# A spacer of 160 bytes in place of 32 on the right of SBUF, and longer durations in a static planner, in attention followed by two expert layers

## Chip, cores and metric

One core of one Trainium2 chip. The metric is the device time of one execution in microseconds, lower is better; three runs of the kernel before gave 1287.57, 1290.01 and 1291.79 us, and their median, 1290.01 us, is the time before.

## Reference

Three layers in a row, all in float32 (8 batches x 8 heads x 576 positions x 64; 4608 tokens, 512 wide):

```python
kv = einsum('bhsd,bhse->bhde', k, v); out = einsum('bhsd,bhde->bhse', q, kv)
x = (out / sqrt(mean(out * out, -1) + 1e-06) * g_norm)      # then heads side by side: 4608 x 512
h = x @ w_in;  g = h * cos(h);  x = g @ w_out               # first layer: 512 -> 2048 -> 512
h = x @ w_in2; solu = h * softmax(h)                        # second layer: 512 -> 1024
x = ((solu - mean(solu)) / sqrt(var(solu) + 1e-06) * g_ln) @ w_out2   # -> 4608 x 512
```

## The kernel before, in words

**Arithmetic.** Every float32 operand of the large products is held as a high and a low part in the format fp32r, side by side in one room, and a product is three matmuls (`mm3`): high by high (L171), high by low (L172), low by high (L173). The part that streams through TensorE, the moving operand, is 512 or 384 columns of 4 bytes; the stationary one is 128 x 128. `split` makes the parts (ACT writes the high one, L394 or L388; DVE or POOL the low one, L395 or L390), `cosine` makes g from h (ACT L667, DVE L669, ACT L672, DVE L674, ACT L676 for the high part, L677 on DVE or POOL for the low one). Inputs that come as pairs of 32-bit words are put together by `convert`: ACT L366, DVE L368, L370, L373, L375, POOL L377 (`either` picks the engine).

**Stages.** Phase 0 is 36 steps: in the gaps of the first quarter of the first layer lie the attention and the conversion of all weights, which go through the staging rooms `ws` out to DRAM (`wid`, `wod`; SP L402, L439). Phase 1 is 15 items, 5 blocks of tokens (384, 384, 512, 512, 512 columns) by the other 3 quarters of the hidden width: `first_h` computes h by seven products (moving operand `rxa` or `rxb`), `first_out` multiplies g (moving operand one of 12 `rg` rooms, taken in turn; rooms 8 to 11 are pieces of `rg2x`) by w_out. Each item's weights come back from DRAM into the left rooms `rwi` (L447) and `rwo` (L453, slots 0 and 1). The tokens of a block come by L726 into `xf`, and `prep` makes sums of them (POOL L627) and splits them into `rxa`/`rxb`. Phase 2 is 18 pairs of token tiles of the second layer; there `rxb` holds weights and is a moving operand too (L857).

**Rooms.** Pools are laid from the left end of SBUF upward (`const`, `rwo`, `rxa`, `rg`, `ws`, `fconv`, `sf`, `xf`, `fh`, then `pa` or `rwi`) and from the right end downward (`edge`, then `att`, later `rxb`, `mid`, `rg2`). `edge` is declared at L197 and opened first; no instruction reads or writes it, so its size only moves the other right rooms. In bytes within a partition the rooms on the left that this text speaks of start at 64 beyond a multiple of 256; `rxb` and `rg2x`, on the right, start at 192 beyond one (`rxb` at 204736, `rg2x` at 176064).

**The order.** Nothing is scheduled on the chip: each engine runs a fixed list. `Flow` collects tasks with an engine, a duration, a due time `at` and what they read and write, and `run` (L121) plays them through a small model. A ready task of the lowest due time goes first; a DMA lands a fixed 2.0 us after its end on the queue (`lat`); and all POOL tasks and all DVE tasks that don't read PSUM share one `port`, so in the plan only one of them runs at a time (L135, L150):

```python
return max(self.free.get(t.eng, 0.0), t.ready, port if t.port else 0.0)
...
if t.port:
    port = t.end
```

The durations are the second argument of each `add`. The order in which tasks start in the plan is the order of the program on every engine and queue, and semaphores make it right whatever the real durations are.

Of the kernel before, what the change touches and what calls it, by code (L numbers as in the profile page):

```python
# [11 lines left out]
U32 = mybir.dt.uint32  # L12
# [5 lines left out]
P = 128  # L18
# [48 lines left out]
class Flow:  # L67
# [13 lines left out]
    def declare(self, pool, tag, n, shape, dt=F32):  # L81

        for key in [(tag, i) for i in range(n)] if n else [tag]:
            self.pool_of[key] = pool
            self.specs.setdefault(pool, []).append((key, shape, dt))
# [18 lines left out]
    def add(self, eng, dur, fn, r=(), w=(), at=0.0, lat=0.0, ps=False):  # L104
        t = Task()
        t.eng, t.dur, t.fn, t.at, t.lat = eng, dur, fn, at, lat
        t.port = eng in ("POOL", "DVE") and not ps
        t.deps, t.next, t.end, t.left, t.seq = set(), [], None, 0, len(self.tasks)
        for k in {*r, *(self.pool_of[k] for k in (*r, *w) if k in self.pool_of)}:
            if k in self.writer:  # L110
                t.deps.add(self.writer[k])
            self.readers.setdefault(k, []).append(t)
        for k in w:
            t.deps.update(self.readers.get(k, ()))
            if k in self.writer:
                t.deps.add(self.writer[k])
            self.writer[k], self.readers[k] = t, []
        t.deps.discard(t)
        self.tasks.append(t)
# [40 lines left out]
def tile_kernel(ctx, tc, qkv, tail, g2, w1, w2, gl, out):  # L160
    nc = tc.nc
    PE, ACT, DVE, POOL, SP = nc.tensor, nc.scalar, nc.vector, nc.gpsimd, nc.sync
    flow = Flow()
    add = flow.add
    buf, declare = flow.buf, flow.declare

    def f(ap):
        return ap.bitcast(F32)
# [25 lines left out]
    declare("const", "ident", 0, [P, P])  # L194
    declare("const", "small", 0, [P, 2 * len(SMALL)])

    declare("edge", "edge", 0, [P, 8])  # L197
    for s in range(2):
        declare("rwi", ("rwi", s), 0, [P, 2 * NOP * 256], F32R)
        declare("rwo", ("rwo", s), 0, [P, 2 * 2 * 512], F32R)  # L200
# [96 lines left out]
    def rx(o, o_to=None):  # L297

        o_to = o + 1 if o_to is None else o_to
        if o < S1:  # L300
            room, at = buf["rxb"][:, 0:4096], o
        elif o == A22:
            room, at = buf["rxb"][:, 4096:6144], 0
        else:
            room, at = buf["rxa", (o - S1) // 2], (o - S1) % 2
        return room.rearrange("p (l c n) -> p l c n", l=2, n=512)[:, :, 2 * at:2 * (at + o_to - o), :]
# [41 lines left out]
    def e_(full, half, n):  # L348
        return half + (full - half) * (n - 256) / 256


    def convert(src, sk, yk, wk, at, load_at, on_dve, wide=1.3):
        def word(i):
            return buf[sk][:, :, i]

        def a():
            return buf[yk].bitcast(U32)

        if isinstance(src, list):
            for i, part in enumerate(src):  # L360
                add("SP", 0.8, lambda i=i, part=part: SP.dma_start(out=buf[sk][:, i * 256:(i + 1) * 256, :], in_=part),
                    r=[sk] if i else [], w=[("half", sk)] if i else [sk, ("half", sk)], at=load_at, lat=2.0)
        else:
            add("SP", 1.6, lambda: SP.dma_start(out=buf[sk], in_=src.rearrange("p (n w) -> p n w", w=2)),
                w=[sk, ("half", sk)], at=load_at, lat=2.0)
        add("ACT", 0.67, lambda: ACT.activation(out=buf[yk], in_=word(1).bitcast(F32), func=AF.Copy, scale=2.0 ** -112),  # L366
            r=[sk, ("half", sk)], w=[yk], at=at)
        add("DVE", 0.43, lambda: DVE.tensor_scalar(out=a(), in0=a(), scalar1=3, scalar2=None,  # L368
                                                   op0=ALU.logical_shift_left), r=[yk], w=[yk], at=at)
        add("DVE", 0.71, lambda: DVE.scalar_tensor_tensor(out=a(), in0=word(1), scalar=0x80000000, in1=a(),  # L370
                                                         op0=ALU.bitwise_and, op1=ALU.bitwise_or),
            r=[yk, sk, ("half", sk)], w=[yk], at=at)
        add("DVE", 0.43, lambda: DVE.tensor_scalar(out=buf[wk].bitcast(U32), in0=a(), scalar1=0xFF800000, scalar2=None,  # L373
                                                   op0=ALU.bitwise_and), r=[yk], w=[wk], at=at)
        add("DVE", 0.71, lambda: DVE.scalar_tensor_tensor(out=buf[wk], in0=word(0), scalar=2.0 ** -52, in1=buf[wk],  # L375
                                                         op0=ALU.mult, op1=ALU.mult), r=[wk, sk, ("half", sk)], w=[wk], at=at)
        either(on_dve, 512, lambda eng: eng.tensor_tensor(out=buf[wk], in0=buf[yk], in1=buf[wk], op=ALU.add),  # L377
               r=[yk, wk], w=[wk], at=at)

    def either(on_dve, n, fn, r, w, at):  # L380
        eng = DVE if on_dve else POOL
        dur = e_(0.8, 0.44, n) if on_dve else e_(1.2, 0.7, n)
        add("DVE" if on_dve else "POOL", dur, lambda: fn(eng), r=r, w=w, at=at)

    def split(src, keys, n, hi, lo, hk, lk, at, on_dve, scale=None):

        if scale is not None:
            add("ACT", 0.66, lambda: ACT.activation(out=hi(), in_=src(), func=AF.Copy, scale=scale()),  # L388
                r=[*keys, "gl"], w=hk, at=at)
            add("DVE", 0.71, lambda: DVE.scalar_tensor_tensor(out=lo(), in0=src(), scalar=scale(), in1=f(hi()),  # L390
                                                             op0=ALU.mult, op1=ALU.subtract),
                r=[*keys, *hk, "gl"], w=lk, at=at)
            return
        add("ACT", 0.64 if n == 512 else 0.42, lambda: ACT.copy(out=hi(), in_=src()), r=keys, w=hk, at=at)  # L394
        either(on_dve, n, lambda eng: eng.tensor_tensor(out=lo(), in0=src(), in1=f(hi()), op=ALU.subtract),  # L395
               [*keys, *hk], lk, at)
# [216 lines left out]
    def prep(src, keys, dst, hk, lk, at, lo_dve):  # L613

        fk = sfs()

        def sf(n, n_to=None):
            return buf[fk][:, 2 * n:2 * (n + 1 if n_to is None else n_to), :]

        def sk(n):  # L620
            return n, fk

        for n in range(4):
            flow.pool_of[sk(n)] = fk

        def op(out_, fn, in0, in1, r, w):
            add("POOL", 0.75, lambda: POOL.tensor_tensor(out=out_(), in0=in0(), in1=in1(), op=fn), r=[*keys, *r], w=w, at=at)  # L627

        a = src
        flow.change(lambda: None, (fk,), ())  # L630
        op(lambda: sf(0), ALU.add, lambda: a(1, 0, 2), lambda: a(1, 2, 4), [], [sk(0)])
        op(lambda: sf(1), ALU.subtract, lambda: sf(0), lambda: a(0, 0, 2), [sk(0)], [sk(1)])
        op(lambda: sf(2), ALU.subtract, lambda: a(0, 0, 2), lambda: a(1, 0, 2), [], [sk(2)])
        op(lambda: sf(3), ALU.subtract, lambda: a(0, 2, 4), lambda: sf(1), [sk(1)], [sk(3)])
        groups = [(0, 2, 512, lambda: a(0, 0, 4), []),
                  (2, 4, 512, lambda: sf(0, 2), [sk(0), sk(1)]),
                  (4, 6, 512, lambda: sf(2, 4), [sk(2), sk(3)]),
                  (6, 7, 256, lambda: a(1, 2, 4), [])]
        for n, (lo, hi, wide, s, r) in enumerate(groups):
            split(s, [*keys, *r], wide, lambda lo=lo, hi=hi: dst(0, lo, hi),  # L640
                  lambda lo=lo, hi=hi: dst(1, lo, hi), [(*hk, o) for o in range(lo, hi)],
                  [(*lk, o) for o in range(lo, hi)], at, lo_dve(n))
# [179 lines left out]
    def place_b(b):  # L822

        return {B11: A11, T2: S2, T1: S1, B21: A12, T3: S3, B22: S4, T4: A22}[b]
# [159 lines left out]
    def t_step(i):  # L984
        return T0 + STEP_A * i
# [7 lines left out]
    for i, (n, c) in enumerate(order):  # L993
        at = t_step(c + 2 * n) - CV_AHEAD
        wk = early_wf[i % 6]
# [64 lines left out]
    for i in range(NSTEP):  # L1060
        m, c = divmod(i, CPP)
        at, d = t_step(i), STEP_A
# [28 lines left out]
    at = T1_  # L1091
    for b, (t0, T) in enumerate(BLOCKS):

        for i, q in enumerate((3, 2, 1) if b % 2 else (1, 2, 3)):
            dur = e_(ITEM, ITEM / 2 + 0.6, T * P)
# [10 lines left out]
    for n, item in enumerate([*items, None]):  # L1106
        at = item["at"] if item else T_E2
        if item:
            T, q, dur = item["T"], item["q"], item["dur"]
# [10 lines left out]
        else:  # L1120
            dur, new = 22.0, True
# [5 lines left out]
            for b in (B11, T2, T1, B21, T3, B22, T4):  # L1127
                for kk in range(2):
                    for part in range(2):
                        add("SP", 0.8, lambda b=b, kk=kk, part=part: SP.dma_start(  # L1130
                            out=f(rx(place_b(b))[:, part, kk, :]).rearrange("p (z n) -> p z n", z=2),
                            in_=bd[:, kk, :, part, b * 256:(b + 1) * 256]),
                            r=[("bd", kk, 0, b), ("bd", kk, 1, b)] + ([("b", b)] if part or kk else []), w=[("b", b)],
                            at=at, lat=2.0)
# [17 lines left out]
    for c in range(NC):  # L1152
        flow.change(lambda: None, (f"rg{c}",), (f"lw{c}",))
        add("SP", 1.6, lambda c=c: SP.dma_start(out=f(rg(c)), in_=lwd[c]), r=[("lwd", c)], w=[("lw", c)],
            at=T_E2 + c, lat=2.0)
    for u in range(NU):
        at = T_E2 + 22 + PAIR_C * u
# [56 lines left out]
```

## Time and profile before

| | |
|---|---|
| median of 3 runs | 1290.01 us |
| profiled execution | 1292.3 us, of which the span is 1290.4 us |
| granted TensorE clock, mean | 0.989 |
| busy share of PE, DVE, ACT, POOL | 97%, 72%, 53%, 40% |
| PE on the chain that ended last | 75% |

All times of the trace count from the start of the span. PE's busy time has the modelled ends of pipelined matmuls in it, so the rate of a stretch is read from the starts of its instructions. A stretch in which PE waits shows in two views: in brackets behind the instruction that waited (the idle time, and the engine and line that ended it), and as busy time under the length of a window.

### The profile page before, as it was taken

How to read it: one execution, taken by the hardware profiler on the slowest of the kernel's cores; microseconds unless marked ns; L12 is line 12 of the kernel's file. 1: busy time of each engine (PE TensorE's matmuls, PEld its weight loads, DVE VectorE, ACT ScalarE, POOL GpSimd, SP SyncE). 2: the span in 40 equal slices, each digit the busy share in tenths (PEclk: the TensorE clock that was granted, in tenths of full speed). 3: DMA queues.
4: the chain of work that ended last, by engine and by line, in shares of the span. 5: the costliest groups of instructions: out<-in, count | busy, mean ns of one | idle time of the engine just before them, and what ended most of it. 6: DMA issues, size and time to landing. Idle time of an engine off the chain costs nothing.

```text
span 1290.4 us, 18723 instructions
## 1 busy us (share of the span) xinstructions
PE 1257.6 (97%) x6576; PEld 1066.5 (83%) x6576; DVE 930.3 (72%) x1544; ACT 677.9 (53%) x1225; POOL 518.3 (40%) x510
## 2 busy tenths in 40 slices
PE   5899999999999999999999999999999999999998
PEld 4688888887999899888788888887888888888887
DVE  6777777777887687878787766565777677776753
ACT  4666766675663563645364534442555545454533
POOL 2246656756745666554543443221321212121000
PEclk8899999999999999999999999999999999999999
DMA  8888899568948858663774374387111111111000
GB/s 278 292 264 283 286 326 304 191 216 282 336 152 227 285 184 276 211 227 115 241 221 157 101 212 136 107 284 237 59 56 50 50 42 56 43 50 42 25 25 33
DMA packets 177406, 224.59 MB, mean 174 GB/s; under 512 B 10912, under 2 KB 115360, under 8 KB 177312
## 3 DMA queue, kind: packets, MB, share of 16 engines
q1 hardware_dynamic: 177312, 223.39, 53.4%
q8 instruction: 52, 0.85, 0.3%
q14 instruction: 42, 0.34, 0.1%
HBM read 156.77 MB, written 66.58 MB: 173 GB/s over the span
## 4 chain that ended last, share of the span: by engine, by line
PE 75%; POOL 3%; DVE 3%; DMA 2%; issue 2%; ACT 1%; SPq 0%; POOLq 0%; ACTq 0%; DVEq 0%
PE ps L171 24%; PE ps L172 24%; PE ps L173 24%; PE ps L932 2%; POOL rg L677 1%; PE ps L552 1%; POOL fconv L419 1%; POOL fconv L377 1%; POOL ws L395 1%; DMA px<-fh 1%; PE ps L589 1%; DMA xf<-xd 0%; DMA bd<-ws 0%; PE ps L495 0%; DMA wid<-ws 0%
## 5 line engine op out<-in xcount | busy, mean ns | idle before, releaser
L171 PE MATMUL ps<-rg,rwo 128*128 128x512 f32 (+1 forms) x912 | 349.5, 383 | 1.6 <-ACT rg L676 1.6
L172 PE MATMUL ps<-rg,rwo 128*128 128x512 f32 (+1 forms) x912 | 346.6, 380 | 1.2 <-POOL rg L677 1.2
L173 PE MATMUL ps<-rg,rwo 128*128 128x512 f32 (+1 forms) x912 | 346.4, 380 | 0.0
L677 POOL TENSOR_TENSOR rg<-fh,rg 128x512 fp32r<-128x512 f32 (+1 forms) x120 | 149.3, 1253 | 174.4 <-ACT rg L676 161.5
L171 PEld LDWEIGHTS ps<-rg,rwo 128*128 128x128 f32 x912 | 171.9, 188 | 30.7 <-ACT rg L676 1.9
L172 PEld LDWEIGHTS ps<-rg,rwo 128*128 128x128 f32 x912 | 171.7, 188 | 30.3 <-POOL rg L677 2.2
L173 PEld LDWEIGHTS ps<-rg,rwo 128*128 128x128 f32 x912 | 171.6, 188 | 29.4
L914 POOL TENSOR_TENSOR const<-const,const 128x1 f32<-128x1 f32 x36 | 20.9, 580 | 333.2 <-DVE const L901 300.0
L171 PE MATMUL ps<-rxa,rwi 128*128 128x512 f32 (+1 forms) x384 | 147.3, 383 | 1.4 <-DVE fh L862 0.8
L172 PE MATMUL ps<-rxa,rwi 128*128 128x512 f32 (+1 forms) x384 | 145.6, 379 | 1.2 <-DVE rxa L395 1.2
L173 PE MATMUL ps<-rxa,rwi 128*128 128x512 f32 (+1 forms) x384 | 145.2, 378 | 0.0
L667 ACT ACTIVATE fh<-ps 128x512 int32<-128x512 f32 (+1 forms) x126 | 71.3, 567 | 103.4 <-PE ps L173 83.3
L672 ACT ACTIVATE fh<-fh,const 128x512 f32<-128x512 f32 (+1 forms) x156 | 106.6, 690 | 32.6 <-DVE fh L669 31.7
L171 PE MATMUL ps<-rxb,rwi 128*128 128x512 f32 (+1 forms) x288 | 112.7, 391 | 4.8 <-DVE fh L757 3.0
L676 ACT CAST rg<-fh 128x512 fp32r<-128x512 f32 (+1 forms) x156 | 90.6, 586 | 41.6 <-DVE fh L674 39.5
L173 PE MATMUL ps<-rxb,rwi 128*128 128x512 f32 (+1 forms) x288 | 110.4, 383 | 0.0
L172 PE MATMUL ps<-rxb,rwi 128*128 128x512 f32 (+1 forms) x288 | 109.9, 381 | 0.0
L669 DVE SCALAR_TENSOR_TENSOR fh<-ps,fh 128x512 f32<-128x512 f32 (+1 forms) x126 | 81.2, 648 | 28.3 <-ACT fh L667 25.6
L674 DVE TENSOR_TENSOR fh<-ps,fh 128x512 f32<-128x512 f32 (+1 forms) x126 | 80.9, 647 | 24.8 <-ACT fh L672 24.5
L627 POOL TENSOR_TENSOR sf<-xf 128x256 f32<-128x256 f32 x72 | 62.6, 876 | 61.9 <-DMA xf<-xd 32.5
L171 PEld LDWEIGHTS ps<-rxa,rwi 128*128 128x128 f32 x384 | 72.5, 189 | 14.5 <-DVE fh L862 1.3
L808 DVE TENSOR_TENSOR mid<-ps,mid 128x512 f32<-128x512 f32 (+1 forms) x90 | 56.9, 633 | 37.7 <-PE ps L173 37.2
(121 smaller groups left out, 2348.4 us busy)
## 6 DMA issues: line engine op xcount, KB each, us to landing
rwi<-wid SPq DMA_DIRECT2D x66, 512.0 KB, 5.7
rwo<-wod SPq DMA_DIRECT2D x88, 256.0 KB, 3.8
fconv<-w SPq DMA_DIRECT2D x36, 512.0 KB, 4.6
att<-qkv SPq DMA_DIRECT2D x32, 512.0 KB, 5.9
px<-fh SPq DMA_DIRECT2D x42, 256.0 KB, 4.2
xd<-xf SPq DMA_DIRECT2D x18, 512.0 KB, 3.9
wid<-ws SPq DMA_DIRECT2D x18, 512.0 KB, 4.7
xf<-xd SPq DMA_DIRECT2D x18, 512.0 KB, 5.2
```

The lines of the kernel that those rows point to most:

```text
L171: PE.matmul(ps, lhsT=lh, rhs=rh, start=start, stop=False, skip_group_check=more)
L172: PE.matmul(ps, lhsT=lh, rhs=rl, start=False, stop=False, skip_group_check=more)
L173: PE.matmul(ps, lhsT=ll, rhs=rh, start=False, stop=stop, skip_group_check=more)
L627: add("POOL", 0.75, lambda: POOL.tensor_tensor(out=out_(), in0=in0(), in1=in1(), op=fn), r=[*keys, *r], w=w, at=at)
L667: add("ACT", e_(0.61, 0.42, n), lambda: ACT.activation(out=tt().bitcast(I32), in_=h(), func=AF.Copy, scale=INV_2PI, bias=0.25), r=r, w=[tk ...
L669: add("DVE", e_(0.71, 0.44, n), lambda: DVE.scalar_tensor_tensor(out=tt(), in0=h(), scalar=INV_2PI, in1=tt().bitcast(I32), op0=ALU.mult, o ...
L672: add("ACT", e_(0.74, 0.5, n), lambda: ACT.activation(out=tt(), in_=tt(), func=AF.Sin, bias=buf["halfpi"][:, 0:1], scale=TWO_PI), r=[tk, " ...
L674: add("DVE", e_(0.71, 0.44, n), lambda: DVE.tensor_tensor(out=tt(), in0=h(), in1=tt(), op=ALU.mult), r=[*r, tk], w=[tk], at=t, ps=psrc)
L676: add("ACT", e_(0.64, 0.42, n), lambda: ACT.copy(out=hi(), in_=tt()), r=[tk], w=hk, at=t + 2)
L677: either(on_dve, n, lambda eng: eng.tensor_tensor(out=lo(), in0=tt(), in1=f(hi()), op=ALU.subtract), [tk, *hk], lk, t + 2)
L808: add("DVE", e_(0.71, 0.44, n), lambda ak=ak, bk=bk: DVE.tensor_tensor(out=buf[ak][:, 0:n], in0=buf[bk][:, 0:n], in1=buf[ak][:, 0:n], op=A ...
L932: PE.transpose(tr()[:, c, :], buf["h2", n][:, (4 * q + c) * P:(4 * q + c + 1) * P], buf["ident"])
```

## The change

Two things, neither of which adds an instruction or changes a sum. `edge` grows from 8 to 40 floats, so every other right room lies 128 bytes lower (`rxb` at 204608, `rg2x` at 175936: 64 beyond a multiple of 256, as on the left). And the planner gets longer durations for DVE L368, L370, L373, for `either` (L377, L395, L419, L677) and for the sums of `prep` (L627).

```diff
-    declare("edge", "edge", 0, [P, 8])                                        # L197
+    declare("edge", "edge", 0, [P, 40])
...
-        add("DVE", 0.43, lambda: DVE.tensor_scalar(out=a(), in0=a(), scalar1=3, scalar2=None,     # L368
+        add("DVE", 0.55, lambda: DVE.tensor_scalar(out=a(), in0=a(), scalar1=3, scalar2=None,
...
-        add("DVE", 0.71, lambda: DVE.scalar_tensor_tensor(out=a(), in0=word(1), scalar=0x80000000, in1=a(),     # L370
+        add("DVE", 0.78, lambda: DVE.scalar_tensor_tensor(out=a(), in0=word(1), scalar=0x80000000, in1=a(),
...
-        add("DVE", 0.43, lambda: DVE.tensor_scalar(out=buf[wk].bitcast(U32), in0=a(), scalar1=0xFF800000, scalar2=None,     # L373
+        add("DVE", 0.48, lambda: DVE.tensor_scalar(out=buf[wk].bitcast(U32), in0=a(), scalar1=0xFF800000, scalar2=None,
...
     def either(on_dve, n, fn, r, w, at):
         eng = DVE if on_dve else POOL
-        dur = e_(0.8, 0.44, n) if on_dve else e_(1.2, 0.7, n)
+        dur = e_(0.82, 0.5, n) if on_dve else e_(1.38, 0.8, n)
...
-            add("POOL", 0.75, lambda: POOL.tensor_tensor(out=out_(), in0=in0(), in1=in1(), op=fn), r=[*keys, *r], w=w, at=at)     # L627
+            add("POOL", 0.9, lambda: POOL.tensor_tensor(out=out_(), in0=in0(), in1=in1(), op=fn), r=[*keys, *r], w=w, at=at)
```

The second part moves instructions on every engine from early in phase 0 to the end of phase 1. Three places, in order of time.

DVE at the start of phase 1's second item, around 320 us (`ps6`, `ps1` are banks of PSUM into which PE next adds; `fconv` is the conversion's room). Before:

```order
L757 TENSOR_TENSOR fh_0_115<-ps0_0_167,fh_0_115 128x384
L757 TENSOR_TENSOR fh_0_115<-ps1_0_171,fh_0_115 128x384
L669 SCALAR_TENSOR_TENSOR fh_0_115<-ps7_0_195,fh_0_115 128x384
L757 TENSOR_TENSOR ps6_0_191<-ps6_0_191,fh_0_115 128x384
L757 TENSOR_TENSOR ps1_0_171<-ps1_0_171,fh_0_115 128x384
L669 SCALAR_TENSOR_TENSOR fh_0_115<-ps6_0_191,fh_0_115 128x384
L669 SCALAR_TENSOR_TENSOR fh_0_115<-ps1_0_171,fh_0_115 128x384
L373 TENSOR_SCALAR fconv_0_101<-fconv_0_101 128x512
L669 SCALAR_TENSOR_TENSOR fh_0_115<-fh_0_115 128x384
L375 SCALAR_TENSOR_TENSOR fconv_0_101<-fconv_0_101 128x512
```

Now:

```order
L669 SCALAR_TENSOR_TENSOR fh_0_115<-ps7_0_195,fh_0_115 128x384
L757 TENSOR_TENSOR fh_0_115<-ps1_0_171,fh_0_115 128x384
L373 TENSOR_SCALAR fconv_0_101<-fconv_0_101 128x512
L757 TENSOR_TENSOR ps6_0_191<-ps6_0_191,fh_0_115 128x384
L757 TENSOR_TENSOR ps1_0_171<-ps1_0_171,fh_0_115 128x384
L669 SCALAR_TENSOR_TENSOR fh_0_115<-ps6_0_191,fh_0_115 128x384
L669 SCALAR_TENSOR_TENSOR fh_0_115<-ps1_0_171,fh_0_115 128x384
L375 SCALAR_TENSOR_TENSOR fconv_0_101<-fconv_0_101 128x512
L669 SCALAR_TENSOR_TENSOR fh_0_115<-fh_0_115 128x384
```

L373, which writes `fconv` and must wait until POOL L395 has read it, now stands ahead of the two L757 that hand `ps6` and `ps1` back to PE, and not behind them.

SP, the last conversion of w_out for the first block, around 392 us (`wod` is written from the staging rooms by L439 and comes back as `rwo` by L453; the two last L439 write what slot 1 then reads). Before:

```order
L361 DMA fconv_0_101<-w1 128x512 x3
L439 DMA wod_60<-ws_1_97 128x4x128 x2
L453 DMA rwo_0_75<-wod_60 128x512
L453 DMA rwo_1_76<-wod_60 128x512
L453 DMA rwo_0_75<-wod_60 128x512
L453 DMA rwo_1_76<-wod_60 128x512
```

Now:

```order
L439 DMA wod_60<-ws_0_96 128x4x128 x2
L453 DMA rwo_0_75<-wod_60 128x512
L361 DMA fconv_0_101<-w1 128x512
L453 DMA rwo_0_75<-wod_60 128x512
L361 DMA fconv_0_101<-w1 128x512
L439 DMA wod_60<-ws_1_97 128x4x128 x2
L453 DMA rwo_1_76<-wod_60 128x512
L726 DMA xf_1_111<-xd_58 128x1024
L453 DMA rwo_1_76<-wod_60 128x512 x3
```

The last pair of L439 stood ahead of all eight reloads (two more pairs of L453 follow there); now it stands behind those of slot 0 and straight ahead of the first reload of slot 1, `rwo_1`. In the combined order PE has 16 matmuls of 384 columns left between the last L439 and its first read of `rwo_1`.

ACT around 421 us, in an item of 384 columns. Before:

```order
L672 ACTIVATE fh_0_115<-fh_0_115,const_1_67 128x384
L667 ACTIVATE fh_0_115<-fh_0_115 128x384
L366 ACTIVATE fconv_0_101<-fconv_0_101 128x512
L676 CAST rg2_0_2491<-fh_0_115 128x384
L667 ACTIVATE fh_0_115<-ps7_0_195 128x384
L667 ACTIVATE fh_0_115<-ps6_0_191 128x384
L769 COPY fh_0_115<-ps0_0_167 128x384
L394 CAST ws_1_97<-fconv_0_101 128x512
L394 CAST ws_0_96<-fconv_0_101 128x512
```

Now:

```order
L672 ACTIVATE fh_0_115<-fh_0_115,const_1_67 128x384
L667 ACTIVATE fh_0_115<-fh_0_115 128x384
L667 ACTIVATE fh_0_115<-ps7_0_195 128x384
L676 CAST rg2_0_2449<-fh_0_115 128x384
L769 COPY fh_0_115<-ps0_0_167 128x384
L667 ACTIVATE fh_0_115<-ps6_0_191 128x384
L672 ACTIVATE fh_0_115<-fh_0_115,const_1_67 128x384 x3
```

The conversion's L366 is gone from ahead of L676, the cast that PE waits for, and the two L394 after it are gone as well; the next L366 now stands ten rows behind that L676.

## Rows read from the trace of the kernel before

**Rows 1.** the page: busy time of each engine, its share of the span, instructions

```profile
PE 1257.6 (97%) x6576; PEld 1066.5 (83%) x6576; DVE 930.3 (72%) x1544; ACT 677.9 (53%) x1225; POOL 518.3 (40%) x510
```

**Rows 2.** waits of PE: who waits for whom, us in total, times, longest

```profile
PE ps L171 <- DVE fh L757: 3.0, 1, 3.0
PE ps L171 <- ACT rg L676: 1.6, 1, 1.6
PE ps L172 <- POOL rg L677: 1.2, 2, 1.0
```

**Rows 3.** timeline of PE, 559 to 572 us: start, duration, instruction (512-wide products)

```profile
559.88 0.39 PE L171 MATMUL ps<-rxa,rwi 128*128 128x512 f32 x1
...
563.28 0.40 PE L171 MATMUL ps<-rxb,rwi 128*128 128x512 f32 x1
...
566.07 0.39 PE L171 MATMUL ps<-rg,rwo 128*128 128x512 f32 x1
...
568.16 0.40 PE L171 MATMUL ps<-rxa,rwi 128*128 128x512 f32 x1
```

**Rows 4.** the same, 413 to 426 us (384-wide products)

```profile
416.31 0.33 PE L171 MATMUL ps<-rxa,rwi 128*128 128x384 f32 x1
...
417.87 0.34 PE L171 MATMUL ps<-rxb,rwi 128*128 128x384 f32 x1
...
419.98 0.34 PE L171 MATMUL ps<-rg,rwo 128*128 128x384 f32 x1
```

**Rows 5.** groups by line and form: count, busy us and mean ns, idle before

```profile
L171 PE MATMUL ps<-rg,rwo 128*128 128x512 f32 x720 | 284.3, 395 | 0.0
...
L171 PE MATMUL ps<-rxb,rwi 128*128 128x512 f32 x216 | 88.1, 408 | 3.0 <-DVE fh L757 3.0
...
L171 PE MATMUL ps<-rg,rwo 128*128 128x384 f32 x192 | 65.1, 339 | 1.6 <-ACT rg L676 1.6
...
L171 PE MATMUL ps<-rxb,rwi 128*128 128x384 f32 x72 | 24.7, 343 | 1.8 <-DVE fh L674 1.2 <-ACT fh L769 0.6
```

**Rows 6.** timeline of PE, 628 to 648 us (in brackets: idle before it)

```profile
637.37 0.40 PE L173 MATMUL ps<-rxb,rwi 128*128 128x512 f32 x1
640.77 0.79 PE L171 MATMUL ps<-rxb,rwi 128*128 128x512 f32 x1 [3.01 <-DVE fh L757]
```

**Rows 7.** windows: length, busy PE, PEld, DVE, ACT, POOL, granted clock, DMA share, GB/s

```profile
307.00:323.00 16.00, 13.00 (x69) 11.46 (x68) 12.35 (x22) 8.54 (x18) 10.34 (x10) 1.00 0.98 303
415.00:426.00 11.00, 8.37 (x44) 7.80 (x43) 6.06 (x11) 5.11 (x11) 10.84 (x12) 0.95 0.75 217
641.00:647.00 6.00, 6.00 (x15) 4.68 (x16) 3.50 (x6) 4.33 (x8) 0.56 (x2) 0.52 1.03 358
```

**Rows 8.** timelines of POOL and of ACT, 628 to 648 us

```profile
632.91 0.74 POOL L627 TENSOR_TENSOR sf<-xf 128x256 f32<-128x256 f32 x1 [3.47 <-DMA xf<-xd]
...
634.93 0.72 ACT L388 ACTIVATE ws<-fconv,const 128x512 fp32r<-128x512 f32 x1 [11.22 <-POOL fconv L377]
```

**Rows 9.** DMA issues: count, KB each, median us from issue to landing

```profile
rwo<-wod SPq DMA_DIRECT2D x88, 256.0 KB, 3.8
...
wid<-ws SPq DMA_DIRECT2D x18, 512.0 KB, 4.7
...
wod<-ws SPq DMA_DIRECT2D x24, 256.0 KB, 4.7
```

**Rows 10.** groups by line and form, of the conversion's small pieces

```profile
L373 DVE TENSOR_SCALAR fconv<-fconv 128x512 uint32<-128x512 uint32 x42 | 23.9, 569 | 6.5 <-POOL ws L395 6.1
...
L395 POOL TENSOR_TENSOR ws<-fconv,ws 128x256 fp32r<-128x256 f32 x10 | 7.4, 737 | 20.1 <-ACT ws L394 20.1
...
L394 ACT CAST ws<-fconv 128x256 fp32r<-128x256 f32 x10 | 4.0, 404 | 13.7 <-DMA bd<-ws 8.5 <-DMA wid<-ws 5.0
```

**Rows 11.** groups by line and form, of L370 in the two conversion rooms

```profile
L370 DVE SCALAR_TENSOR_TENSOR fconv<-fconv 128x512 uint32<-128x512 uint32 x42 | 33.9, 808 | 0.5
...
L370 DVE SCALAR_TENSOR_TENSOR pa<-pa,pa 128x512 uint32<-128x512 uint32 x2 | 1.4, 690 | 0.0
```

## Prediction

> **What bounds the kernel.** I read the busy times first: PE works 1257.6 of 1290.4 us [rows 1], so 32.8 us of idleness is all that a better order can win, and two levers are left: what one matmul takes, and the few places where PE waits. The waits of PE between 300 us and the end are single events [rows 2]: one wait of 3.0 us for DVE L757, one of 1.6 us for ACT L676, one of 1.0 us for POOL L677. Then I read, from the starts of matmuls, what one takes. At 560 us 15 matmuls with `rxa` as moving operand start in 3.40 us, 227 ns each; the next 12, with `rxb`, take 2.79 us, 232.5 ns each; the 9 behind them take 2.09 us, 232 ns each, though not all of those read a room on the right [rows 3]. With 384 columns it is 1.56 us for 9 of `rxa`, 173 ns each, and 2.11 us for 12 of `rxb`, 176 ns each [rows 4]. So a moving operand from the right costs 2.5% or 1.5% more, and for a few matmuls after it the rate stays low.
>
> **The spacer.** It moves the right rooms from 192 to 64 beyond a multiple of 256 bytes, where the left ones lie. If the place within 256 bytes makes the difference, every right matmul falls to the left rate. How many are there? `rxb` has 216 per line with 512 columns and 72 with 384, on three lines: 648 and 216. Of `rg`, phase 1 has 864 matmuls of 512 columns and 576 of 384 (192 per line on three lines) [rows 5]; the twelve rooms are taken in turn and four are on the right, a third: 288 and 192. The last block of phase 0 reads its tokens from `rg2x`, 48 more. That is 984 x 5.8 ns = 5.7 us and 408 x 2.5 ns = 1.0 us; for the matmuls that stay slow after them I add an estimated 1.3 us (some 220 at 5.8 ns: a few after each right stretch, as in [rows 3]). Term: **-8.0 us**; bounds 0, if the place is not the cause, and -10, if more trail behind.
>
> **The order: what goes.** At 637 us DVE stands in L390, which waits for the conversion's ACT L388; L388 idled 11.22 us behind POOL L377, which stood behind a `prep` sum L627 that waited 3.47 us for its tokens [rows 8]. PE's next matmul starts 3.40 us after the one before it instead of 0.23, so 3.2 us are lost [rows 6]; then 15 matmuls in 6 us at a granted clock of 0.52, the lower of the two levels, instead of 3.4 us, 2.6 more [rows 7]. Now L390 is not near that place and L377 stands on the other side of the wait: **-5.8** (bounds -5.8 and 0, if the next late conversion takes its place). At 421 us L366 and the L677 behind it cost 11 - 8.37 = 2.6 us of PE, and the clock there is 0.95, 0.5 more [rows 7]; the conversion has moved away: **-3.1** (bounds -3.1 and 0).
>
> **The order: what comes.** The longer durations raise the load of the planner's common port for POOL and DVE. The trace's means hold waiting for the other engine: L370 takes 808 ns in the room `fconv`, when POOL converts too, and 690 ns in `pa` [rows 11]. The plan already keeps the two apart, so that time is counted twice; conversion work is planned later, and nearer to its due.
>
> First, 307 to 323 us. PE loses 16 - 13 = 3.0 us there already [rows 7]. Now L373 stands ahead of the two L757. It waits for a POOL L395 of 256 columns, that for ACT L394, and this for the landing of a `wid` transfer out of the staging room, 4.7 us after its issue [rows 9]; such waits cost POOL 20.1 us over ten pieces before, off the path [rows 10]. From that issue to the point where PE needs `ps6`, PE has 20 matmuls of 173 ns in the combined order, 3.5 us. So PE waits 4.7 - 3.5 + 0.40 + 0.74 + 0.57 [rows 10] and an L757 of about 0.55, an estimate from L373 itself: 3.5 us. An L677 on DVE that moved behind L669 and L368 ahead of the first products costs up to 2.5 us more, an estimate from three DVE steps near 0.6 each and ACT between them. A pause of that length is followed at 641 us by 2.6 us of loss from the clock; half of it here, since the pieces are shorter: 1.3. Together 3.5 + 2.5 + 1.3 beside what is lost now: **+7.3** (bounds 0, if DMA lands early, and +10).
>
> Second, 392 us, where PE never waited. The last L439 is issued 16 matmuls of 173 ns, 2.8 us, before PE's first read of `rwo_1`; it lands after 4.7 us, and only then can the reload be issued, which lands after 3.8 [rows 9]. PE waits 4.7 + 3.8 - 2.8 = 5.7 us, and then runs at the lower clock; 2.3 us of that by the nearest row, the 2.6 at 641 us: **+8.0** (bounds 0, if the conversion runs ahead of the plan, and +9).
>
> Third, late in phase 0, an L394 of 256 columns now waits for a `wid` landing ahead of the ACT copies that free PE's banks; 4.7 us [rows 9], of which the matmuls between cover most: **+1.0** (bounds 0 and +3.5). Everything else that moved I cost at nothing: it lies on DVE, ACT or POOL, which are idle 28%, 47% and 60% of the time [rows 1]; where that cover is gone, a wait like the ones above appears, up to 3 us each.
>
> **Sum.** -8.0 - 5.8 - 3.1 + 7.3 + 8.0 + 1.0 = -0.6 us. The profiled execution of 1292.3 us becomes 1291.7; it stood 2.3 us above the median of 1290.0, and against that the forecast is **1289.4 us**. Two large gains and two large losses cancel nearly; a measurement of this kernel tells about 0.3%, 3.9 us, from no change.
>
> **Rivals.** *The new waits mostly don't come* (faster). Each rests on a DMA landing at its median and on an engine that is as late as the plan has it; the plan before also took 2.0 us for transfers that need 3.8 to 4.7 [rows 9], and yet PE waited at few places [rows 2]. If half of the 16.3 us comes, the sum is -8.8: 1281 us. It speaks against this that both places put a transfer and its reader within 3.5 us of PE's work.
>
> *The place within 256 bytes does nothing* (slower). Left and right rooms also differ in how high they lie, and in that `rxb` and `rg2x` lie beside the sums that DVE writes in `mid`; in the trace all left rooms have one place and all right rooms the other, so it can't be split there. The matmuls of [rows 3] that read left rooms at the slow rate behind `rxb` speak a little for this. Price: the -8.0 is gone, the sum +7.4, 1297 us; it decides as soon as less than 3.5 of the 8 us come, which is right matmuls above 230 ns. The Trainium skill, in "SBUF — State Buffer", section "Specifications (TRN2)", gives lines of 16 bytes within which an access costs no more, and "SBUF: two separate sides" says that TensorE's port waits for nobody; by these, both spacers being multiples of 16, the move changes nothing and the time is this rival's. The 232.5 against 227 ns show that some difference between the rooms exists which those sentences don't name.
>
> *Neither part does what it says*: no gain from the rooms, and few of the new waits. Then -8.9 from what goes and +8 from what comes: within 0.3%.
>
> **Numbers.** Forecast (rooms gain, new waits come) 0.36; new waits mostly missing 0.30; rooms gain nothing 0.20; neither 0.10; a wait elsewhere that I have not seen 0.04. Faster by over 0.3%, under 1286.1: the second, and a tenth of the first, 0.34. Slower, over 1293.9: the third, the last, and 0.03 of the first, 0.27. The rest, 0.39, is within. The forecast's own range is 1285 to 1295; with the rivals, and the bounds of the two large new waits, 1278 to 1300.
>
> **What would show it.** Right matmuls (`rxb`, late `rg`) at 227 and 173 ns between starts; no wait of PE for L757 at the old 637 us and none at 421 us; a wait of PE on L171 to L173 for `rwo<-wod` near 392 us, followed by a stretch at a clock near 0.5; more than 3 us lost around 320 us. The prediction is wrong if `rxb` stays at 232 ns, or if PE passes 392 us without a pause.

## Result and the profile after

The change made the kernel slower: 1296.87 us (median of 6 runs, 1294.03 to 1298.25) against 1289.22 us for the kernel before (6 runs), a ratio of 1.0063 with a 95% interval of 1.0046 to 1.0079, so 8 us more. The forecast was 1289.4 us and no change that can be measured. The profiled execution has a span of 1295.3 us and a granted clock of 0.986 (before 1290.4 us and 0.989).

The busy times, which answer to [rows 1], and the waits of PE, which answer to [rows 2]:

```profile
PE 1250.2 (97%) x6576; PEld 1067.8 (82%) x6576; DVE 927.6 (72%) x1544; ACT 679.4 (52%) x1225; POOL 518.9 (40%) x510
```

```profile
PE ps L589 <- DVE att L584: 6.3, 5, 2.0
PE ps L171 <- DMA rwo<-wod: 6.2, 2, 3.5
PE ps L171 <- DVE fh L674: 5.9, 1, 5.9
...
PE ps L172 <- DVE rg L677: 2.9, 1, 2.9
PE ps L172 <- POOL rg L677: 2.1, 1, 2.1
PE ps L552 <- ACT xf L593: 1.7, 2, 0.8
PE ps L495 <- ACT xf L593: 1.6, 2, 0.8
```

PE is busy 7.4 us less than before although the span is 4.9 us longer: the matmuls became faster, the waits more. The wait of 3.0 us for L757 is gone. New, or far longer than before, are one of 5.9 us for L674, two for `rwo<-wod` of up to 3.5 us, two for L677 of 2.9 and 2.1 us, and four small ones for ACT L593.

How fast the matmuls became is read from the starts of PE's instructions (start, duration), as in [rows 3]:

```profile
575.32 0.39 PE L171 MATMUL ps<-rxa,rwi 128*128 128x512 f32 x1
...
578.04 0.39 PE L171 MATMUL ps<-rg,rwo 128*128 128x512 f32 x1
...
580.76 0.39 PE L171 MATMUL ps<-rxb,rwi 128*128 128x512 f32 x1
...
583.48 0.39 PE L171 MATMUL ps<-rg,rwo 128*128 128x512 f32 x1
```

Each of the three stretches has 12 matmuls in 2.72 us, 226.7 ns each. `rxb`, on the right, now runs like `rxa`; it took 232.5 ns before.

Where PE lost time, in windows that answer to [rows 7] (the same columns), all four of the changed kernel: at the first attention tiles, around the first item of phase 1, at the reads of `rwo`, and over the stretch in which PE had stopped at 637 us:

```profile
70.00:90.00 20.00, 16.97 (x144) 13.94 (x142) 13.64 (x24) 11.61 (x21) 6.42 (x6) 0.83 0.65 210
305.00:345.00 40.00, 27.82 (x133) 24.60 (x132) 23.65 (x36) 18.36 (x37) 27.66 (x28) 0.91 0.82 264
405.00:418.00 13.00, 6.80 (x30) 5.90 (x29) 9.32 (x13) 0.92 (x2) 6.90 (x8) 0.77 0.65 227
...
620.00:660.00 40.00, 40.00 (x178) 33.15 (x177) 31.66 (x47) 14.43 (x26) 21.52 (x21) 1.00 0.88 271
```

In the kernel before, the first of these windows was almost full, and the clock in it was whole:

```profile
70.00:90.00 20.00, 19.85 (x170) 16.11 (x169) 15.91 (x27) 14.54 (x28) 5.92 (x6) 1.00 0.78 248
```

To compare kernels whose instructions stand in another order, I worked out a **loss by stage** from the starts of PE's matmuls: the time from each start to the next, less 226.7 ns (512 columns) or 173.4 ns (384) for a matmul of L171 to L173; the rest, the attention's matmuls and the transposes included, counts whole. Stages end at the same number of matmuls of L171 to L173 in every kernel; the times in the head of the table are those of the kernel before. One traced execution each, in us; it can lie some us from the median of its kernel (e5 3.6 below, e2 3.4 and the kernel before 3.1 above), so a difference of 1 or 2 us in the table says little:

| kernel | to 86 us | to 290 | to 333 | to 403 | to 436 | to 799 | to the end | sum |
|---|---|---|---|---|---|---|---|---|
| before | 53.1 | 49.4 | 4.9 | 1.2 | 4.9 | 11.7 | 37.5 | 162.8 |
| changed | 60.5 | 47.6 | 15.9 | 9.2 | 0.0 | 0.1 | 34.7 | 168.0 |
| e1 spacer alone | 53.0 | 49.2 | 4.7 | 0.3 | 2.5 | 7.6 | 34.4 | 151.8 |
| e2 durations alone | 60.5 | 47.9 | 16.8 | 8.8 | 0.2 | 4.6 | 37.9 | 176.8 |
| e5 only `prep` | 53.1 | 49.2 | 8.7 | 0.0 | 0.0 | 7.1 | 34.7 | 152.7 |
| e6 only DVE | 54.9 | 52.2 | 15.7 | 0.0 | 0.0 | 2.1 | 34.4 | 159.2 |
| e7 only `either` | 55.5 | 49.7 | 10.9 | 2.9 | 0.0 | 2.2 | 34.6 | 155.8 |
| e8 no port | 58.3 | 54.2 | 5.2 | 2.4 | 7.7 | 2.5 | 37.3 | 167.7 |
| e9 late only | 53.8 | 49.1 | 4.8 | 0.2 | 0.0 | 2.5 | 34.7 | 145.1 |
| e10 first eight old | 53.4 | 48.8 | 21.9 | 8.3 | 0.0 | 0.1 | 34.7 | 167.2 |
| e11 from item two | 53.6 | 49.3 | 7.9 | 0.9 | 3.9 | 1.0 | 34.7 | 151.3 |

### The profile page after: what moved, and what is told of

It reads as the page before. It is cut to its first block, busy times and chain, and to the rows that moved or that the text cites. A ratio compares the mean times of both kernels' runs of the same rounds, so it can differ in the third digit from the quotient of the medians.

```text
span 1295.3 us, 18726 instructions
## 1 busy us (share of the span) xinstructions
PE 1250.2 (97%) x6576; PEld 1067.8 (82%) x6576; DVE 927.6 (72%) x1544; ACT 679.4 (52%) x1225; POOL 518.9 (40%) x510
## 4 chain that ended last, share of the span: by engine, by line
PE 91%; DVE 2%; DMA 2%; POOL 2%; ACT 2%; issue 1%; SPq 1%; ACTq 0%; DVEq 0%; POOLq 0%
PE ps L171 28%; PE ps L172 28%; PE ps L173 28%; PE ps L932 2%; PE ps L552 2%; PE ps L495 2%; PE ps L589 1%; POOL att L570 1%; DMA att<-qkv 1%; DMA rwo<-wod 0%; DMA xf<-xd 0%; DMA wod<-ws 0%; POOL att L569 0%; DVE att L562 0%; DVE fh L669 0%
## 5 line engine op out<-in xcount | busy, mean ns | idle before, releaser
L171 PE MATMUL ps<-rg,rwo 128*128 128x512 f32 (+1 forms) x912 | 349.1, 383 | 6.2 <-DMA rwo<-wod 6.2
L173 PE MATMUL ps<-rg,rwo 128*128 128x512 f32 (+1 forms) x912 | 345.5, 379 | 0.0
L677 POOL TENSOR_TENSOR rg<-fh,rg 128x512 fp32r<-128x512 f32 (+1 forms) x120 | 148.8, 1255 | 148.5 <-ACT rg L676 123.6
L171 PEld LDWEIGHTS ps<-rg,rwo 128*128 128x128 f32 x912 | 172.0, 189 | 34.8 <-issue 3.7
L173 PEld LDWEIGHTS ps<-rg,rwo 128*128 128x128 f32 x912 | 171.9, 188 | 28.4
L171 PE MATMUL ps<-rxa,rwi 128*128 128x512 f32 (+1 forms) x384 | 146.6, 382 | 2.1 <-DVE fh L862 1.0
L173 PE MATMUL ps<-rxa,rwi 128*128 128x512 f32 (+1 forms) x384 | 144.7, 377 | 0.0
L672 ACT ACTIVATE fh<-fh,const 128x512 f32<-128x512 f32 (+1 forms) x156 | 105.7, 689 | 41.5 <-DVE fh L669 40.9
L676 ACT CAST rg<-fh 128x512 fp32r<-128x512 f32 (+1 forms) x156 | 89.8, 585 | 52.4 <-DVE fh L674 49.9
L171 PE MATMUL ps<-rxb,rwi 128*128 128x512 f32 (+1 forms) x288 | 111.2, 386 | 5.9 <-DVE fh L674 5.9
L172 PE MATMUL ps<-rxb,rwi 128*128 128x512 f32 (+1 forms) x288 | 108.7, 377 | 0.0
L173 PE MATMUL ps<-rxb,rwi 128*128 128x512 f32 (+1 forms) x288 | 108.7, 377 | 0.0
L669 DVE SCALAR_TENSOR_TENSOR fh<-ps,fh 128x512 f32<-128x512 f32 (+1 forms) x126 | 80.9, 648 | 30.5 <-ACT fh L667 28.8
L674 DVE TENSOR_TENSOR fh<-ps,fh 128x512 f32<-128x512 f32 (+1 forms) x126 | 80.8, 646 | 20.5 <-ACT fh L672 20.0
L395 POOL TENSOR_TENSOR ws<-fconv,ws 128x512 fp32r<-128x512 f32 (+1 forms) x52 | 67.1, 1298 | 51.7 <-ACT ws L394 41.9
L377 POOL TENSOR_TENSOR fconv<-fconv 128x512 f32<-128x512 f32 x40 | 54.0, 1350 | 83.4 <-DVE fconv L375 81.2
```

What stands on the lines that cost most here:

```text
L171: PE.matmul(ps, lhsT=lh, rhs=rh, start=start, stop=False, skip_group_check=more)
L172: PE.matmul(ps, lhsT=lh, rhs=rl, start=False, stop=False, skip_group_check=more)
L173: PE.matmul(ps, lhsT=ll, rhs=rh, start=False, stop=stop, skip_group_check=more)
L669: add("DVE", e_(0.71, 0.44, n), lambda: DVE.scalar_tensor_tensor(out=tt(), in0=h(), scalar=INV_2PI, in1=tt().bitcast(I32), op0=ALU.mult, o ...
L672: add("ACT", e_(0.74, 0.5, n), lambda: ACT.activation(out=tt(), in_=tt(), func=AF.Sin, bias=buf["halfpi"][:, 0:1], scale=TWO_PI), r=[tk, " ...
L674: add("DVE", e_(0.71, 0.44, n), lambda: DVE.tensor_tensor(out=tt(), in0=h(), in1=tt(), op=ALU.mult), r=[*r, tk], w=[tk], at=t, ps=psrc)
```

## Experiments

After the result I held this theory: the spacer gains its 8 us, and the new order loses about twice that, because the conversion of the weights slips behind its use. The rivals: the spacer does nothing or brings waits of its own, or any other set of durations shuffles the order at such a price.

### The two halves apart

Spacer alone:

```diff
-    declare("edge", "edge", 0, [P, 8])
+    declare("edge", "edge", 0, [P, 40])
```

> The spacer of 160 bytes with the old durations; the order of the program is that of before. Theory (the spacer gains, the new order costs more): right matmuls at 227 and 173 ns, about 8 us under before, 1281 us; the waits at 320, 421 and 637 us stay. Rival (the spacer itself brings waits in the changed kernel, and the order costs little): within 3 us of before or slower.

Measured: 1281.0 us against 1287.8, ratio 0.9947 (0.9926 to 0.9968). The 12 `rxb` matmuls from 560.62 us on take 2.72 us, 226.7 ns each.

Durations alone (all the other lines of the change):

> The new durations with the spacer of 32 bytes. Theory: the order alone costs 12 to 14 us, so about 1302 us, with the waits near 311, 330, 407 and 412 us of the changed kernel and right matmuls at 232 ns. Rival (the order is about neutral): 1287 to 1293 us.

Measured: 1302.54 us, ratio 1.0119 (1.0099 to 1.0138). So by the medians the spacer is worth -6.8 us and the order +14.7; their sum, 7.9, is what the change as a whole costs (8 us). The traces say the same of the rate in either order: summed over all matmuls of L171 to L173 that are followed within 260 ns by another, what goes beyond 226.7 or 173.4 ns is 10.7 us before and 2.1 with the spacer alone, 10.9 with the durations alone and 2.5 in the changed kernel. The theory holds, both rivals on the spacer fall, and what was mis-sized is the order, a little above the 12 to 14 us expected here too.

### What the spacer does: alike, not where

All left rooms moved up by 128 bytes too, and the spacer left as it was, so that everything starts at 192 beyond a multiple of 256:

```diff
-    declare("const", "small", 0, [P, 2 * len(SMALL)])
+    declare("const", "small", 0, [P, 2 * len(SMALL)]); declare("const", "shift", 0, [P, 32])
```

> The spacer as before, and 128 bytes more at the left end, so that left and right rooms all start at 192 beyond a multiple of 256. Theory A (the place of the moving operand itself sets the rate): the left matmuls slow down to 232 and 176 ns too, some 3000 x 5.8 ns and 600 x 2.5 ns, 19 us, about 1308 us. Theory B (what counts is that moving and stationary operand lie alike): all matmuls at 227 and 173 ns, 8 us under before, 1281 us.

Measured: 1278.71 us, ratio 0.9934 (0.9914 to 0.9953). Theory A would have made the left matmuls slow; PE's starts show every room at the fast rate (12 matmuls in each of the stretches that begin at 571.31 and 576.75 us, 2.72 us each):

```profile
571.31 0.39 PE L171 MATMUL ps<-rxa,rwi 128*128 128x512 f32 x1
...
574.03 0.39 PE L171 MATMUL ps<-rg,rwo 128*128 128x512 f32 x1
...
576.75 0.39 PE L171 MATMUL ps<-rxb,rwi 128*128 128x512 f32 x1
...
579.47 0.39 PE L171 MATMUL ps<-rxa,rwi 128*128 128x512 f32 x1
```

The place of the moving operand by itself is thus not the cause: 192 is slow while the left rooms, the stationary operands among them, lie at 64, and fast when they lie at 192 too. A spacer of 96 bytes, between the two, with the old durations:

```diff
-    declare("edge", "edge", 0, [P, 8])
+    declare("edge", "edge", 0, [P, 24])
```

> A spacer of 96 bytes, old durations: right rooms at 128 beyond a multiple of 256. Theory A or B with a cost that grows with the distance: right matmuls between 227 and 232 ns, 1283 to 1287 us. If only one place is fast: 232 ns still, 1289 us. If only one place is slow: 227 ns, 1281 us.

Measured: 1289.92 us, ratio 1.0019 (1.0007 to 1.0031): no gain at all, though the rooms are now only 64 bytes off.

```profile
572.65 0.40 PE L171 MATMUL ps<-rxa,rwi 128*128 128x512 f32 x1
...
575.41 0.39 PE L171 MATMUL ps<-rg,rwo 128*128 128x512 f32 x1
...
578.19 0.40 PE L171 MATMUL ps<-rxb,rwi 128*128 128x512 f32 x1
...
580.99 0.40 PE L171 MATMUL ps<-rxa,rwi 128*128 128x512 f32 x1
```

Here 12 matmuls take 2.76, 2.78 and 2.80 us: `rxb` still 233 ns, `rxa` 230, and the `rg` rooms, of which some lie on the right, 232. The sum beyond 226.7 and 173.4 ns is 11.7 us, no less than before.

Theory B, as it was put, is not shown by this. `rxa` is slow here although it and its stationary operand both lie at 64, and it takes about 231 ns in places before too (six matmuls from 588.65 to 590.04 us). With 384 columns it even changes sides: in phase 1 `rxb` takes 173.4 ns on average with this spacer and `rxa` 175.2, where it was 176.2 and 174.2 before. What is shown is that every stretch is fast when all rooms lie alike, and that right rooms 64 or 128 bytes off slow their own matmuls or the left ones behind them. Whether a moving operand must lie like its stationary one or like the moving operand before it was not separated, since the shift moved all left rooms at once.

### Which duration costs what

With the spacer of 160 bytes, one group of new durations at a time. Only `prep`:

```diff
-            add("POOL", 0.75, lambda: POOL.tensor_tensor(out=out_(), in0=in0(), in1=in1(), op=fn), r=[*keys, *r], w=w, at=at)
+            add("POOL", 0.9, lambda: POOL.tensor_tensor(out=out_(), in0=in0(), in1=in1(), op=fn), r=[*keys, *r], w=w, at=at)
```

> Spacer of 160 bytes; of the durations only that of the sums of prep (L627) is new. In the order the conversion's last L439 stands where it stood before. Theory (the order costs because the conversion slips behind its use): no wait on rwo near 400 us, at most a few us lost at the start of phase 1, 1281 to 1284 us. Rival (any new set of durations shuffles the order and costs about alike): 1287 us or more.

Measured: 1285.4 us, ratio 0.9971 (0.9951 to 0.9992).

Only the three DVE durations of `convert` (0.43, 0.71, 0.43 to 0.55, 0.78, 0.48):

> Spacer of 160 bytes; only the durations of DVE L368, L370, L373 are new. The conversion's last L439 stands 59 matmuls later than before, still some 95 ahead of the first read of rwo_1. Theory (slip): no wait on rwo near 400 us, part of the loss at 311 to 341 us, 1283 to 1289 us. Rival (any new set costs alike): 1292 us or more.

Measured: 1290.1 us, ratio 1.0014 (0.9999 to 1.003).

Only `either`:

```diff
-        dur = e_(0.8, 0.44, n) if on_dve else e_(1.2, 0.7, n)
+        dur = e_(0.82, 0.5, n) if on_dve else e_(1.38, 0.8, n)
```

> Spacer of 160 bytes; only the durations of either (L377, L395, L419, L677) are new. The last L439 stands 62 matmuls later than before. Theory (slip): no wait on rwo near 400 us, part of the loss at 311 to 341 us, 1283 to 1290 us. Rival (any new set costs alike): 1292 us or more. If the small waits near 55 and 75 us come from these durations, 6 us of loss appear before 110 us here and not in the run with the DVE durations alone.

Measured: 1286.21 us, ratio 0.9987 (0.9974 to 1.0001). All three ratios lie above that of the spacer alone, that of `prep` by less than the intervals tell apart; the first two times lie above what the theory expected, by 1.4 and 1.1 us, and none reaches the rival's 1287 or 1292 us. In the order, the conversion's last L439 stands after 1802 matmuls before, 1801 with `prep` alone, 1861 and 1864 with one of the others, and 1941 with all. The table shows what each position costs. The wait on `rwo` near 400 us is there only at 1941 (with the spacer, without it, and in the run with the first eight old durations below). The loss from 290 to 333 us is 8.7 us without slip and 10.9 to 15.7 us with 60. So the first goes with the slip alone; the second has a part (4.0 us over the spacer alone) that comes with the longer `prep` and no slip. The last condition in the expectation for `either` failed: with the DVE durations alone PE waits for L593 four times (4.2 us), with `either` alone twice (1.4 us), and up to 86 us these two kernels lose 1.9 and 2.5 us more than the spacer alone, not 6.

### Is it the time counted twice?

The changed kernel, but the planner has no common port for POOL and DVE:

```diff
-        t.port = eng in ("POOL", "DVE") and not ps
+        t.port = False
```

> The changed kernel, but the planner lets POOL and DVE run at the same time (no common port). The conversion's last L439 stands 319 matmuls earlier than in the changed kernel, 180 earlier than before. Theory (longer durations do harm because the plan already keeps the two engines apart and so counts the time twice; the conversion slips): the waits at 330 and 407 us vanish and the time falls to 1276 to 1286 us. Rival (the port is what keeps the order realistic): DVE and POOL late nearly everywhere, new waits of PE, 1297 us or more.

Measured: 1298.86 us, ratio 1.0075 (1.0053 to 1.0096). Both halves of the expectation came true in places. The conversion comes 319 matmuls earlier, there is no wait on `rwo`, and the loss from 290 to 333 us falls from 15.9 to 5.2 us, though `prep` is as long as in the changed kernel: with the conversion out of the way the stage is cheap. But now other waits stand elsewhere:

```profile
PE ps L171 <- DVE fh L674: 8.3, 9, 3.1
...
PE ps L171 <- DVE fh L757: 4.1, 3, 3.0
```

From 86 to 290 us the loss is 54.2 instead of 47.6 us, and from 403 to 436 us 7.7 instead of nothing. PE now waits for DVE in twelve places of these two kinds. The longest for L674, 3.11 us, ends at 273.73 us, and the clock from 273 to 281 us is 0.79: that is most of what late phase 0 loses here beyond the spacer alone (5.0 us). I take it that a plan in which the two engines never hinder each other has DVE too early nearly everywhere; this was not shown. That the time counted twice is the whole cause isn't borne out: the port is a coarse picture, and with no port the plan is no better.

### Late only, and the early part

New durations only for tasks due after 430 us in the plan, in each of the five places in this way:

```diff
-        add("DVE", 0.55, lambda: DVE.tensor_scalar(out=a(), in0=a(), scalar1=3, scalar2=None,
+        add("DVE", 0.55 if at > 430 else 0.43, lambda: DVE.tensor_scalar(out=a(), in0=a(), scalar1=3, scalar2=None,
```

> Spacer of 160 bytes; the new durations only for tasks due after 430 us in the plan (from phase 1's fourth item on), the old ones before. Theory (the harm of the new durations lies in phase 0 and the first items, where the conversion slips; later they take waits away): losses as with the spacer alone up to 400 us, and from there on almost none, as in the changed kernel: 1270 to 1276 us. Rival (the later part has no waits only because the conversion arrives in it late): waits near 421 and 637 us as before, 1280 us or more.

Measured: 1273.49 us against 1286.92, ratio 0.9888 (0.9868 to 0.9909): faster than both kernels. Of PE's waits for DVE, ACT and POOL in phase 1 these are the largest, none over 1.8 us:

```profile
PE ps L172 <- POOL rg L677: 1.8, 1, 1.8
PE ps L172 <- DVE rxa L395: 1.2, 2, 0.9
PE ps L171 <- DVE fh L674: 1.2, 1, 1.2
```

The rival fell: from 403 to 799 us this kernel loses 2.5 us where the spacer alone loses 10.1, although nothing in it arrives earlier: the last L439 for the first block stands after 1802 matmuls, as before, and many conversions behind that stand later than before, some by over 200 matmuls.

The changed kernel with the old durations for the first eight conversions (`0.43 if on_dve else 0.55` and the like, and `either` on DVE with its old values up to 60 us):

> The changed kernel with the old durations for the first eight conversions alone (those that DVE does, before 60 us); PE's order up to 70 us is that of before again, but the conversion stands about 45 matmuls later still at 1000 matmuls. Theory (the waits for ACT L593 near 51 and 75 us come from the order of the first attention tiles, which these eight durations move): 6 to 7 us less lost before 110 us, 1288 to 1292 us. Rival (the early loss comes from the conversion being late as such): no gain, 1295 us or more.

Measured: 1295.94 us, ratio 1.0064 (1.0042 to 1.0086). The mechanism was right and the sum was not: the loss to 86 us falls from 60.5 to 53.4 us, and the waits for L593 are gone, but that from 290 to 333 us grows from 15.9 to 21.9 us. The conversion stands up to some 90 matmuls later than in the changed kernel until there, and no later from there on (1941 in both); that this slip makes the 6.0 us is likely, but no run separates it. Three waits there are 14.0 us:

```profile
313.21 0.69 PE L171 MATMUL ps<-rxa,rwi 128*128 128x384 f32 x1 [4.54 <-ACT rxa L394]
315.43 0.69 PE L172 MATMUL ps<-rxa,rwi 128*128 128x384 f32 x1 [1.53 <-DVE rxa L395]
335.14 0.69 PE L171 MATMUL ps<-rxb,rwi 128*128 128x384 f32 x1 [7.97 <-DVE fh L674]
```

As the late-only kernel, but from 370 us:

> As the run before the last, but the new durations from 370 us of the plan on (second item), so they also set the order around 392 to 421 us. The conversion's last L439 stands 154 matmuls earlier than in the changed kernel. Theory (slip): no wait on rwo near 400 us; a new loss only where L373 now stands ahead of an L757: 1270 to 1279 us. Rival (new durations bring the wait on rwo wherever they are used): 6 us or more lost near 400 us, 1280 us or more.

Measured: 1279.17 us, ratio 0.9924 (0.99 to 0.9947). That is the upper end of the theory's range. There is no wait on `rwo`, as the theory has it, and 3.9 us are lost near 421 us. From 290 to 333 us it loses 3.2 us more than the spacer alone, but not as expected: L373 stands ahead of one L757 and runs there in 0.41 us without waiting. What grew are PE's waits for L395, L674 and L769 (1.50, 1.73 and 0.71 us), with a clock of 0.83 from 320 to 330 us.

## Why the prediction was wrong, point by point

**The spacer: right in size, the reason open.** The term was -8.0 us. The runs gave -6.8 (interval -9.5 to -4.1), and the rate came out as forecast: 226.7 ns. That the right rooms had to come to the place of the left ones was the right guess, but their place alone is not the cause, as the shift on the left showed. One reading was off without harm: of the 15 matmuls that the prediction gives to `rxa` from 559.88 us on, 12 read `rg` rooms. The rival that the move does nothing falls. By the Trainium skill, "SBUF — State Buffer", sections "Specifications (TRN2)", with its lines of 16 bytes, and "SBUF: two separate sides", where PE never waits on another, the time would have been that rival's. Both spacers are multiples of 16 bytes, and yet the right matmuls take 232.5 ns with the one and 226.7 ns with the other, so here the measurement decides.

**What goes: right.** 637 us was to give 5.8 us and 421 us 3.1. From 436 to 799 us the changed kernel loses 0.1 us and the spacer alone 7.6; from 403 to 436 us it is 0.0 and 2.5. The 7.6 are not all one stop: with the spacer alone PE waits 2.05 us there, with clock 3.8 us lost, and the rest are smaller waits that went too.

**392 us, the reload of `rwo`: right in place and about in size.** The queue of SP and PE in the changed kernel:

```profile
403.19 1.31 SPq L439 DMA_DIRECT2D wod<-ws  x2
...
408.34 0.33 SPq L453 DMA_DIRECT2D rwo<-wod  x1
...
411.07 0.41 PE L171 MATMUL ps<-rg,rwo 128*128 128x384 f32 x1 [3.45 <-DMA rwo<-wod]
415.22 0.69 PE L171 MATMUL ps<-rg,rwo 128*128 128x384 f32 x1 [2.75 <-DMA rwo<-wod]
```

L453 can be issued 5.15 us after the first L439, and PE waits 3.45 and 2.75 us, 6.2 where I had 5.7. Beside the spacer alone, the stage loses 8.9 us more; the term was +8.0.

**307 to 323 us: right in place, wrong on what ends the wait.** The term was +7.3 us, and the stage lost 15.9 - 4.7 = 11.2 more. The chain starts as forecast, here on ACT, DVE and PE:

```profile
328.63 0.41 ACT L394 CAST ws<-fconv 128x256 fp32r<-128x256 f32 x1 [4.12 <-DMA wid<-ws]
...
329.94 0.94 DVE L373 TENSOR_SCALAR fconv<-fconv 128x512 uint32<-128x512 uint32 x1 [3.11 <-POOL ws L395]
330.80 1.02 DVE L757 TENSOR_TENSOR ps<-ps,fh 128x384 f32<-128x384 f32 x2
...
335.71 1.06 DVE L674 TENSOR_TENSOR fh<-ps,fh 128x384 f32<-128x384 f32 x2 [1.19 <-ACT fh L672]
...
336.33 0.69 PE L171 MATMUL ps<-rxb,rwi 128*128 128x384 f32 x1 [5.93 <-DVE fh L674]
```

I let the wait end with L757, and the section on the change says that the two L757 hand `ps6` and `ps1` back to PE. They don't: L757 writes its sum into `ps6`, `cosine` reads it there, and PE's next matmul, which writes `ps6`, waited, by the profile, for L674. Between L757 and L674 stood three L669 and ACT's L672: from the end of L373 at 330.88 us to PE's start 5.45 us passed, and I had counted 0.55 for them. The kernel before showed it already, in [rows 5] and here; I had left this wait out of the list of single events:

```profile
322.40 0.44 PE L171 MATMUL ps<-rxb,rwi 128*128 128x384 f32 x1 [1.20 <-DVE fh L674]
```

With `prep` alone longer, the same matmul waits 3.54 us for L674, the longest of these three waits, though L373 stands behind both L757 and doesn't wait:

```profile
PE ps L171 <- DVE fh L674: 6.5, 3, 3.5
```

So of the 5.93 us some 3.5 are the chain behind L757 and some 2.4 the wait that was forecast, an estimate from these two runs. Other pieces were the waits for L677 of 2.87 us on DVE, which I had put at up to 2.5, and of 2.12 on POOL, which I hadn't seen. The single run shows that this stage costs some 4 us more by the longer `prep` alone.

**"Everything else that moved I cost at nothing": the step that failed.** The first attention tiles lost 60.5 - 53.0 = 7.5 us more before 86 us, and nothing in the sum stood for that (up to 290 us 1.6 of it came back); a wait in a place not seen had a chance of 0.04, at up to 3 us each. PE there, before:

```profile
73.23 0.83 PE L552 MATMUL ps<-att,att 128*128 128x128 f32 x6
73.82 0.48 PE L171 MATMUL ps<-rg,rwo 128*128 128x512 f32 x1
...
79.02 0.63 PE L589 MATMUL ps<-const,att 128*128 128x128 f32 x4
79.41 0.48 PE L171 MATMUL ps<-rxa,rg 128*128 128x512 f32 x1
...
80.43 1.39 PE L495 MATMUL ps<-att 128*64 128x64 f32 x40
```

Now:

```profile
72.86 0.39 PE L173 MATMUL ps<-rxa,rg 128*128 128x512 f32 x1
73.09 0.60 PE L589 MATMUL ps<-const,att 128*128 128x128 f32 x4
74.52 1.16 PE L552 MATMUL ps<-att,att 128*128 128x128 f32 x8 [0.83 <-ACT xf L593]
77.10 0.66 PE L589 MATMUL ps<-const,att 128*128 128x128 f32 x4 [1.42 <-DVE att L584]
78.53 2.40 PE L495 MATMUL ps<-att 128*64 128x64 f32 x40 [0.78 <-ACT xf L593]
80.87 0.80 PE L171 MATMUL ps<-rxa,rg 128*128 128x512 f32 x1
```

Before, large products stand between the attention's steps. Now, from 72.86 to 80.87 us, no matmul of L171 to L173 starts: the transposes L589, the L552 that needs a bank which ACT L593 must empty first, the next L589 and an L495 stand one behind the other, and each waits for the step before it on another engine. PE waits 3.0 us in pieces, and the clock of the window is 0.83 where it was 1.00. The run with the first eight old durations shows the cause: they alone put PE's order back, and 7.1 us come back with it. I had argued from idle shares over the whole span, 28% to 60%; in the new order PE's list has nothing else between two steps of this chain, and an idle engine doesn't shorten a chain.

**The sum.** By stage, the changed kernel against the spacer alone: +7.5 - 1.6 + 11.2 + 8.9 - 2.5 - 7.5 + 0.3 = +16.3 us, where the terms of the order made +7.4. Of the 8.9 us between them 7.5 lie in the stage that wasn't costed and 3.9 in the one that was mis-sized; the +1.0 for late phase 0 came out as -1.6, and the rest nearly cancels. The rival with the wrong reason (the spacer does nothing, 1297 us) had the time almost to the microsecond: the time alone would have confirmed it, and the start of one `rxb` matmul refutes it.

**What stays open.** Which rooms must lie alike, and why, is not known. Why DVE comes late at 273.73 us in the kernel without the port was not followed. Whether rooms that differ by 256 bytes are alike wasn't tried: there is no room left for such a shift.

## What to carry to other kernels

In a static order one late piece of background work can cost more than all the rest gains: before trusting new durations, look where the last transfer of each background chain now stands against its first reader, and price a wait through to the instruction that frees PE's bank, not to the first one behind it. Durations measured under contention may be right for the stage in which they were measured and wrong elsewhere; here the same numbers gained 7.6 us from 403 to 799 us when used only late (together with the spacer 1273.49 us), and used everywhere they lost 26 us before 403 us. And measure a rate from starts, by operand and place, before and after: it separates a gain from the loss that hides it.

## What the runs showed of the hardware

With all rooms alike within 256 bytes (all at 64, or all at 192), matmuls of 512 columns of 4 bytes started 226.7 ns apart. With the right rooms 128 or 64 bytes off, `rxb` took 232.4 and 230.9 ns on average in phase 1, and `rxa` on the left, behind it, 228.3 and 229.9; over the whole program that came to 8.6 and 9.6 us more than with the spacer of 160 bytes. It costs nothing to mend: the spacer of 160 bytes or the 128 bytes on the left alone gave -0.53% and -0.66%. I had expected a rule of the single operand, if any.

The granted clock was lower behind the longer pauses: 0.77 in the window of the `rwo` waits, 0.83 at the first tiles, and 0.52 in six us at 641 us before, where it had cost nearly as much (2.6 us) as the pause itself (3.2 us). Behind the 1.79 us that the late-only kernel waits for L677 at 522.91 us it stayed at 1.00.
